# A small weight matrix at the head of a fused scan and mixture-of-adapters kernel: loaded in 64-byte pieces, or in 8 rows and transposed on TensorE

## The chip, the cores and the metric

One core of one Trainium2 chip. The metric is the device time of one execution in microseconds (us); lower is better. The profiled execution is one more run of the same program.

## What is computed

The reference, cut to what matters. `a` and `b` are 8 x 6400 x 128; the result of the scan is 51200 rows of 128, and each row goes through the two best of eight low-rank adapters.

```python
def _attn_ref(a, b):                      # a, b: (8, 6400, 128)
    for t in range(S):
        h = a[:, t] * h + b[:, t]
        out[:, t] = h

def _moe_ref(x, w_gate, A, B):            # x: (51200, 128), w_gate: (128, 8)
    logits = x @ w_gate                   # A: (8, 128, 16), B: (8, 16, 128)
    topk = np.argpartition(-logits, K, axis=1)[:, :K]      # K = 2
    ...                                   # w: softmax over the two
    for e in range(E):
        for k in range(K):
            mask = topk[:, k] == e
            z = x[mask] @ A[e]
            delta[mask] += w[mask, k, None] * (z @ B[e])
    return x + delta
```

## The kernel before

The 51200 rows are cut into 100 units of 512. One unit v goes through these steps; the names are those of the kernel's plan:

- `AB{v}` (line 86, TensorE): `a` and `b` of the unit are transposed in fp32 against `ident_f` into PSUM (`pA`, `pB`), so that time runs along the free axis. Units 0 and 1 and the last are special: where a tile is loaded alone, four 128x128 transposes do what eight 64-row transposes do elsewhere, and the `a` part is then a step of its own, `A{v}`, in front of the `b` part.
- `aev{v}` (line 491, ScalarE): `pA` is copied to SBUF.
- `scan{v}` (line 510, VectorE): the recurrence, 512 steps for 128 channels at once, out in fp16 into the ring `xT`.
- `L{v}` (line 82, into `pTL`): logits, four matmuls against the fp16 gate weights. `lev`, `mx` (MAX8, line 589), `p1` to `p7`, `sig`: the gate of a group of one to four units, on ScalarE, VectorE and GpSimd.
- `Z{v}` (line 82, into `pZ`): four matmuls against `Acat_h`, moe_A as one 128x128 fp16 matrix (row d, column e*16+r).
- `mul{v}` (line 729), `T{v}` (line 86), `tev{v}` (line 786): z times its gate, transposed, copied back.
- `R{v}` and `D{v}` (line 82, into `pO`): x itself through `ident_h`, and the adapters' second matrix `Bcat_h`, summed in PSUM. `oev{v}` (line 821): copied to SBUF, then stored.

SyncE (SP) issues all loads of `a` and `b` and all stores; ScalarE's queue issues the three small loads of the weights (`ld_g`, `ld_A`, `ld_B`, by `cst_load`). The casts of the weights to fp16 (`cstg`, `cstA`, `cstB`) run on GpSimd. At the start TensorE has nothing to do until the first tile lands; `heat` gives it seven 512-column matmuls on zeros, and `fill0` three more behind unit 0's transposes.

The order on each engine is fixed when the program is built. `_Plan.schedule` keeps for every step a cost (time on the engine, time to its end) and what it depends on, and goes through the engines in planned time: at each turn the engine that can start soonest takes, among its steps that can start within a small slack (20 ns on TensorE and VectorE, 0 on ScalarE), the one with the smallest key. The key is the unit's number plus an offset for the kind of step: -228.9 for `AB`, -12.2 for `L`, 27.8 for `Z`, 83.5 for the gate, 140.1 for `scan`; steps of the kind `fix` have their number alone (-109 to -105 for the set-up, 1000 for the filler). A change of the tile mode on TensorE ("half", "full") is planned at 94 ns. So a cost or a dependency changed in one place can change the order on all engines behind it. Waits on semaphores follow from the dependencies, also for one step of an engine on an earlier one of the same engine.

TensorE's program is cut into parts by `_Parts`: the first holds 172 entries, each later one 243; a matmul or transpose counts as two. At a cut the engine's sequencer branches to the next part.

Of the kernel before, what the change touches and what calls it, by code (L numbers as in the profile page):

```python
# [91 lines left out]
class _Plan:  # L92
# [9 lines left out]
    def add(self, name, eng, kind, unit, cost, emit, deps=(), dma=None, bank=None, mode=None):  # L102

        engs = (eng,) if isinstance(eng, str) else eng
        cost = cost if isinstance(cost, dict) else {e: cost for e in engs}
        self.ops[name] = _Op(name, engs, kind, unit, cost, emit, list(deps), dma, bank, mode)
# [98 lines left out]
def bass_associative_scan_2x2__then__mixture_of_adapters_kernel(  # L205
# [9 lines left out]
    E = moe_w_gate.shape[1]  # L215
    R = moe_A.shape[2]
# [33 lines left out]
    with ExitStack() as stack:  # L250
        sb = stack.enter_context

        ident_f = sb(nc.sbuf_tensor("ident_f", [128, 128], F32))
        ident_h = sb(nc.sbuf_tensor("ident_h", [128, 128], F16))
        cst_f = sb(nc.sbuf_tensor("cst_f", [128, E + 256], F32))
# [4 lines left out]
        Acat_h = cst_h[:, E : E + 128]  # L260
# [5 lines left out]
        A_e = sb(nc.sbuf_tensor("A_e", [E, D * R], F32))  # L266
# [25 lines left out]
        pZ = [sb(nc.psum_tensor(f"pZ{i}", [128, UT], F32)) for i in range(NZ)]  # L292
# [7 lines left out]
        add = plan.add  # L300

        def add_dma(name, eng, unit, starts, slot, time, deps=()):
# [6 lines left out]
            def emit(h):  # L309
# [18 lines left out]
                fill=1.0,  # L328
# [7 lines left out]
        def cst_load(name, dst, src, after):  # L336

            sem = sb(nc.semaphore(f"s_{name}"))
            add(
                name,  # L340
                "act",
                "fix",
                -109,
                (450.0, 0.0),
                lambda h: h.dma_start(dst, src).then_inc(sem, 16),
                after,
                (sem, 16, 100.0),
            )

        cst_load("ld_g", cst_f[:, 0:E], moe_w_gate[:, :], [])  # L350
        cst_load(
            "ld_A",
            cst_f[:, E : E + 128].rearrange("d (e r) -> d e r", e=E),
            moe_A.rearrange("e d r -> d e r"),
            [],
        )
        cst_load("ld_B", cst_f[:, E + 128 : E + 256], moe_B.rearrange("e r d -> (e r) d"), [])
        add("w0", "dve", "fix", -109, (60.0, 200.0), lambda h: h.memset(warm[:, :], 0.0))
        add("table", "act", "fix", -108, (1500.0, 1600.0), lambda h: h.activation(warm[:, :], warm[:, :], ACTF.Sigmoid), ["w0"])
# [9 lines left out]
        def fill(w):  # L369


            def emit(h):
                for _ in range(3):
                    last = h.matmul(pO[1][:, :], warm_t[:, 0:128], warm_t[:, :])
                return last

            add(f"fill{w}", "pe", "fix", 1000.0, (600.0, 800.0), emit, [f"AB{w}"])

        for w in range(FILLS):
            fill(w)  # L380
        add("idh", "dve", "fix", -108, (150.0, 330.0), lambda h: h.tensor_copy(ident_h[:, :], ident_f[:, :]), ["id"])
        add("cstg", "pool", "fix", -108, (190.0, 290.0), lambda h: h.tensor_copy(wg_h, cst_f[:, 0:E]), ["ld_g"])
        add(
            "cstA",
            "pool",
            "fix",
            -107,
            (290.0, 390.0),
            lambda h: h.tensor_copy(Acat_h, cst_f[:, E : E + 128]),
            ["ld_A"],  # L390
        )
        add(
            "cstB",
            "pool",
# [532 lines left out]
```

## Time and profile before

| | |
|---|---|
| median of 3 runs | 204.48 us (204.47 to 204.71) |
| profiled execution | 204.28 us |
| its span in the profile | 202.5 us |
| TensorE, VectorE, ScalarE, GpSimd busy | 191.0, 184.7, 174.0, 115.7 us |
| granted TensorE clock | 1.00 |
| HBM traffic | 78.8 MB, 389 GB/s over the span |

The profiled execution's own time is 1.8 us longer than its span, since what lies ahead of the first and behind the last instruction is not in the span. In the rows of the profile, PE is TensorE's matmul, PEld its weight load, DVE is VectorE, ACT ScalarE, POOL GpSimd, SP SyncE; a q behind the name is the engine's queue. A timeline row gives start, duration, engine, line, operation, out<-in, shapes, count, and in brackets the idle time in front and what ended it.

### The profile page before, as it was taken

What the parts mean: (1) busy time and instruction counts of PE and PEld (TensorE: products, weight loads), DVE (VectorE), ACT (ScalarE), POOL (GpSimd) and SP (SyncE); (2) the same over time, 40 slices, a digit from 0 to 9 for tenths busy, and PEclk for the clock granted to TensorE, in tenths of its full rate; (3) what the DMA queues carried; (4) which work ended last, traced back from release to release, by engine and by line L of the source; (5) the groups of instructions that cost most, each with busy time, mean ns of one, the idle gap of its engine ahead of it and who ended that gap; (6) DMA issues with size and microseconds to landing.
All of it is one profiled execution on the core that took longest, in us unless ns stands there. A gap on an engine that the chain in (4) does not pass through costs nothing.

```text
span 202.5 us, 8763 instructions
## 1 busy us (share of the span) xinstructions
PE 191.0 (94%) x3594; PEld 171.4 (85%) x3594; DVE 184.7 (91%) x268; ACT 174.0 (86%) x383; POOL 115.7 (57%) x244
## 2 busy tenths in 40 slices
PE   7888988899999999999999999999999999999982
PEld 3666777789899999999999999999999999998981
DVE  1699989999999999999999999999999999988970
ACT  2366775969999999999999999999999999999882
POOL 1325337668467565656746656565674687865620
PEclk9999999999999999999999999999999999999999
DMA  7999999999999999999999999999999999988866
GB/s 185 401 408 409 406 408 406 403 406 411 403 413 414 410 419 409 409 411 414 412 416 409 414 413 411 411 415 415 409 412 414 413 414 410 385 350 350 324 271 263
DMA packets 23687, 79.35 MB, mean 392 GB/s; under 512 B 3680, under 2 KB 3808, under 8 KB 23648
## 3 DMA queue, kind: packets, MB, share of 16 engines
q1 hardware_dynamic: 22320, 78.65, 97.3%
q8 instruction: 29, 0.48, 1.0%
q10 hardware_dynamic: 1328, 0.14, 0.5%
q14 instruction: 10, 0.08, 0.1%
HBM read 52.56 MB, written 26.21 MB: 389 GB/s over the span
## 4 chain that ended last, share of the span: by engine, by line
PE 84%; ACT 6%; DVE 5%; issue 2%; POOL 1%; DVEq 0%
PE pA L86 27%; PE pO L82 23%; PE pTL L86 14%; PE pZ L82 10%; PE pTL L82 5%; DVE xT L510 4%; PE pB L86 4%; ACT a_st L491 2%; ACT outt L821 2%; PE pB L82 2%; ACT zwT L786 1%; DVE mx L589 1%; ACT Lg L583 0%; ACT z_sb L715 0%; POOL pn L632 0%
## 5 line engine op out<-in xcount | busy, mean ns | idle before, releaser
L510 DVE TENSOR_TENSOR_SCAN xT<-a_st,xT,pB 128x512 f16<-128x512 f32 x96 | 120.1, 1251 | 3.2 <-ACT zwT L786 0.5
L491 ACT COPY a_st<-pA 128x512 f32<-128x512 f32 x100 | 60.6, 606 | 19.2 <-PE pB L86 14.6
L86 PE MATMUL pA<-ident_f,a_in 64*128 64x64 f32 (+1 forms) x792 | 71.8, 230 | 2.5 <-ACT a_st L491 0.7
L86 PE MATMUL pB<-ident_f,b_in 64*128 64x64 f32 (+1 forms) x792 | 71.9, 230 | 0.3 <-issue 0.2
L86 PEld LDWEIGHTS pA<-ident_f,a_in 64*128 64x128 f32 (+1 forms) x792 | 57.9, 139 | 10.9 <-ACT a_st L491 1.9
L821 ACT COPY outt<-pO 128x512 f32<-128x512 f32 x96 | 59.5, 626 | 1.9 <-PE pO L82 1.7
L786 ACT COPY zwT<-pTL 128x512 f16<-128x512 f16 x95 | 58.4, 615 | 1.0 <-PE pTL L86 1.0
L86 PEld LDWEIGHTS pB<-ident_f,b_in 64*128 64x128 f32 (+1 forms) x792 | 57.5, 138 | 1.0 <-issue 0.7
L729 DVE TENSOR_TENSOR zw<-pZ,g 128x512 f16<-128x512 f32 x79 | 53.2, 679 | 2.4 <-PE pTL L86 1.4
L82 PE MATMUL pO<-ident_h,xT 128*128 128x128 f16 x400 | 40.8, 227 | 0.9 <-ACT outt L821 0.9
L86 PE MATMUL pTL<-ident_h,zw 128*128 128x128 f16 x380 | 37.8, 221 | 0.5 <-ACT zwT L786 0.4
L82 PE MATMUL pZ<-cst_h,xT 128*128 128x128 f16 x400 | 38.1, 219 | 0.0
L82 PE MATMUL pO<-cst_h,zwT 128*128 128x128 f16 x400 | 36.8, 218 | 0.5 <-ACT zwT L786 0.4
L82 PEld LDWEIGHTS pO<-ident_h,xT 128*128 128x128 f16 x400 | 32.5, 147 | 1.5 <-ACT outt L821 1.2
L729 POOL TENSOR_TENSOR zw<-z_sb,g 128x512 f16<-128x512 f32 x21 | 22.3, 1060 | 17.8 <-PE pTL L82 17.3
L82 PE MATMUL pTL<-cst_h,xT 128*128 128x8 f16 x400 | 27.5, 174 | 1.4 <-DVE xT L510 1.3
L82 PEld LDWEIGHTS pZ<-cst_h,xT 128*128 128x128 f16 x400 | 27.8, 114 | 0.1
L86 PEld LDWEIGHTS pTL<-ident_h,zw 128*128 128x128 f16 x380 | 21.8, 98 | 6.7 <-ACT zwT L786 0.5
L625 POOL TENSOR_TENSOR d<-Lg,m 128x128 f32<-128x128 f32 (+3 forms) x29 | 10.7, 369 | 26.6 <-DVE m L618 26.5
L82 PEld LDWEIGHTS pTL<-cst_h,xT 128*128 128x128 f16 x400 | 23.5, 117 | 2.6 <-DVE xT L510 2.0
L82 PEld LDWEIGHTS pO<-cst_h,zwT 128*128 128x128 f16 x400 | 23.8, 98 | 1.0 <-PE pO L82 0.9
L660 POOL TENSOR_SCALAR pn<-d 128x128 f32<-128x128 f32 (+3 forms) x31 | 17.3, 557 | 2.7
(38 smaller groups left out, 138.3 us busy)
## 6 DMA issues: line engine op xcount, KB each, us to landing
a_in<-in_a_dram SPq DMA_DIRECT2D x49, 512.0 KB, 14.4
b_in<-in_b_dram SPq DMA_DIRECT2D x49, 512.0 KB, 14.2
out_dram<-outt SPq DMA_DIRECT2D x47, 512.0 KB, 13.9
out_dram<-outt SPq DMA_DIRECT2D x6, 256.0 KB, 3.0
a_in<-in_a_dram SPq DMA_DIRECT2D x2, 256.0 KB, 9.1
b_in<-in_b_dram SPq DMA_DIRECT2D x2, 256.0 KB, 4.1
cst_f<-in_moe_A_dram ACTq DMA_DIRECT2D x1, 64.0 KB, 4.2
cst_f<-in_moe_B_dram ACTq DMA_DIRECT2D x1, 64.0 KB, 4.9
```

Of the source, the lines that this page charges most:

```text
L82: return self.h.matmul(*args, **kw)
L86: return self.h.transpose(*args)
L491: lambda h: h.copy(a_st[w % 2][:, :], pA[0][:, :]),
L510: last = h.tensor_tensor_scan(out=x_at(lo, hi), data0=a_st[w % 2][:, lo:hi], data1=pB[w % 2][:, lo:hi], initial=init, op0=ALU.mult, op1=AL ...
L589: last = h.max(mx[s][:, j, :], Lg[s][:, j, :])
L625: lambda h: h.tensor_tensor(out=v(d1[s]), in0=v(Lg[s]), in1=bc(m1[s]), op=ALU.subtract),
L660: lambda h: h.tensor_scalar(v(pn[s]), v(d2[s]), 0.0, -1.0e30, ALU.is_lt, ALU.mult),
L729: lambda h: h.tensor_tensor(out=oview, in0=zview, in1=gview, op=ALU.mult),
L786: lambda h: h.copy(*evacuated(v)),
L821: return copy(outt[:, v % NOUT, :], pO[v % NO][:, :])
```

## The change

moe_A is (8, 128, 16). Before, one DMA puts it straight into place as 128 rows by (e, r), in pieces of 16 floats (64 bytes), and GpSimd casts it. Now the DMA brings it as it lies, 8 rows of 2048 floats, into `A_e` (which both kernels declare), and TensorE transposes, for each r, the 8 x 128 slice with stride 16 into a 128 x 8 slice of `pZ[1]`, again with stride 16 (`arrange`, step `cstT`). The step waits for `ld_A`, the identity and unit 0's last transpose (`AB0`), and has the tile mode "few". VectorE casts the result from PSUM into `Acat_h`. The filler `fill0` has one matmul instead of three, and its planned cost goes from 600 to 200 ns.

```diff
         cst_load("ld_g", cst_f[:, 0:E], moe_w_gate[:, :], [])
-        cst_load(
-            "ld_A",
-            cst_f[:, E : E + 128].rearrange("d (e r) -> d e r", e=E),
-            moe_A.rearrange("e d r -> d e r"),
-            [],
-        )
+        cst_load("ld_A", A_e[:, :], moe_A.rearrange("e d r -> e (d r)"), [])
...
             def emit(h):
-                for _ in range(3):
+                for _ in range(1):
                     last = h.matmul(pO[1][:, :], warm_t[:, 0:128], warm_t[:, :])
                 return last
 
-            add(f"fill{w}", "pe", "fix", 1000.0, (600.0, 800.0), emit, [f"AB{w}"])
+            add(f"fill{w}", "pe", "fix", 1000.0, (200.0, 300.0), emit, [f"AB{w}"])
...
-        add(
-            "cstA",
-            "pool",
-            "fix",
-            -107,
-            (290.0, 390.0),
-            lambda h: h.tensor_copy(Acat_h, cst_f[:, E : E + 128]),
-            ["ld_A"],
-        )
+        def arrange(h):
+            dst = pZ[1][:, 0:128].rearrange("d (e r) -> d r e", e=E)
+            src = A_e[:, :].rearrange("e (d r) -> e r d", r=R)
+            for r in range(R):
+                last = h.transpose(dst[:, r, :], src[:, r, :], ident_f[0:E, 0:E])
+            return last
+
+        add("cstT", "pe", "fix", -105, (600.0, 700.0), arrange, ["ld_A", "id", "AB0"], mode="few")
+        add("cstA", "dve", "fix", -107, (150.0, 330.0), lambda h: h.tensor_copy(Acat_h, pZ[1][:, 0:128]), ["cstT"])
```

## The prediction

> **What bounds the kernel now.** I read the page first (busy shares, the chain that ended last), then the busy time by stretch, then who waited for whom, then the timeline of the first 12 us, where the whole change lies.
>
> ```profile
> span 202.5 us, 8763 instructions
> PE 191.0 (94%) x3594; PEld 171.4 (85%) x3594; DVE 184.7 (91%) x268; ACT 174.0 (86%) x383; POOL 115.7 (57%) x244
> PE 84%; ACT 6%; DVE 5%; issue 2%; POOL 1%; DVEq 0%
> ...
> 10.00:57.00 47.00, 42.34 (x810) 36.72 (x808) 45.40 (x74) 35.86 (x81) 25.34 (x58) 1.00 1.03 407
> 57.00:180.00 123.00, 122.91 (x2444) 113.56 (x2444) 120.12 (x162) 117.86 (x261) 79.87 (x155) 1.00 1.02 410
> ```
>
> In a stretch row the columns after its length are busy PE, PEld, DVE, ACT and POOL, then clock, DMA share and GB/s. From 57 to 180 us PE has no hole (122.91 of 123.00). From 10 to 57 it has 4.7 us of holes, and there VectorE (DVE) is the fullest engine, 45.40 of 47.00. So two engines take turns as the bound, both close to full: whatever makes DVE start its unbroken run later makes PE start its own later too, and nothing behind has room to make it up except the few stops that DVE still has:
>
> ```profile
> DVE mx L589 <- ACT Lg L583: 1.0, 1, 1.0
> DVE xT L510 <- ACT zwT L786: 0.5, 1, 0.5
> DVE zw L729 <- PE pTL L86: 0.2, 1, 0.2
> DVE xT L510 <- PE pO L82: 0.2, 1, 0.2
> ```
>
> These are all of DVE's waits from 8 to 57 us: 1.0 at the very start (it is in front of the first MAX8) and 0.9 in three stops later. DMA is full too (share 1.03), but no row of the waits from 8 us on has a PE that waits for a DMA.
>
> The head, PE first, then DVE:
>
> ```profile
> 4.18 0.94 PE L86 MATMUL pA<-ident_f,a_in 128*128 128x128 f32 x4
> 5.27 0.63 PE L86 MATMUL pB<-ident_f,b_in 128*128 128x128 f32 x4
> 5.96 0.82 PE L82 MATMUL pO<-warm_t 128*128 128x512 f16 x3
> 6.19 0.59 PE L82 MATMUL pO<-warm_t 128*128 128x512 f16 x2
> 6.40 0.38 PE L82 MATMUL pO<-warm_t 128*128 128x512 f16 x1
> 6.71 0.57 PEld L86 LDWEIGHTS pA<-ident_f,a_in 64*128 64x128 f32 x8 [0.42 <-issue]
> 6.71 0.71 PE L86 MATMUL pA<-ident_f,a_in 64*128 64x64 f32 x8
> 7.35 0.29 PE L82 MATMUL pTL<-cst_h,xT 128*128 128x8 f16 x4
> 7.57 0.63 PE L86 MATMUL pB<-ident_f,b_in 128*128 128x128 f32 x4
> 8.03 0.39 PE L82 MATMUL pZ<-cst_h,xT 128*128 128x128 f16 x4
> 8.26 0.39 PE L82 MATMUL pO<-ident_h,xT 128*128 128x128 f16 x4
> ...
> 5.94 1.22 DVE L510 TENSOR_TENSOR_SCAN xT<-a_st,pB 128x512 f16<-128x512 f32 x1 [4.21 <-PE pB L86]
> 8.16 0.37 DVE L589 MAX8 mx<-Lg 128x8 f32<-128x8 f32 x4 [1.00 <-ACT Lg L583]
> 8.45 1.26 DVE L510 TENSOR_TENSOR_SCAN xT<-a_st,xT,pB 128x512 f16<-128x512 f32 x1
> ```
>
> The chain reads: unit 0's b transposes (5.27 to 5.90), three fillers, unit 1's a transposes (6.71, in the text A1), unit 0's logits, unit 1's b transposes (B1, to 8.20), then scan 1. The three fillers start 0.21 apart (5.96 in the longer rows, 6.19, 6.40), and A1 starts 0.31 behind the third: 0.21 of matmul and about 0.1 that I put down to the change of tile size. A1 is held by PE alone: its data had landed.
>
> ```profile
> 1.65 0.42 SPq L311 DMA_DIRECT2D a_in<-in_a_dram  x1
> ...
> a_in<-in_a_dram SPq DMA_DIRECT2D x1, 512.0 KB, 4.7
> cst_f<-in_moe_A_dram ACTq DMA_DIRECT2D x1, 64.0 KB, 4.2
> ...
> DMA packets 1109, 0.26 MB, mean 262 GB/s; under 512 B 1048, under 2 KB 1048, under 8 KB 1109
> q10 hardware_dynamic: 1032, 0.07, 70.7%
> ...
> 5.45 0.29 POOL L389 CAST cst_h<-cst_f 128x128 f16<-128x128 f32 x1 [1.47 <-DMA cst_f<-in_moe_A_dram]
> ```
>
> Issued at 1.65, landed 4.7 later: 6.35, against A1 at 6.71.
>
> **The change part by part.**
>
> *The load of moe_A.* The packet rows are for 3.5 to 4.5 us: queue 10 moves 1032 packets, nearly all moe_A's 64-byte pieces, and they take 70.7% of 16 engines for 1.0 us, 0.71 us. Eight rows of 8 KB are the same 64 KB; at the 407 GB/s of the stretch row that is 0.16 us, or 0.32 if only half of the engines work on it. So the loads behind it land 0.4 to 0.55 us sooner. I value that at nothing: A1's data was there at 6.35 and is now there sooner, and later PE does not wait for loads. moe_A itself landed by 5.45; the transposes can start only behind unit 0's, at 5.96, so even the old landing would do. One issue on ACT's queue stays one issue.
>
> *Fillers, three to one.* Takes 2 x 0.21 = 0.42 us off PE between unit 0 and A1.
>
> *Sixteen transposes.* They wait for unit 0's last transpose, as the first filler does now, so they start at 5.96; by the planner's costs the remaining filler follows them and A1 follows that. Queued behind them on PE: A1, the logits of unit 0, B1, and so everything. The price of one is not in the trace (8 rows, 8 columns moving, fp32, weights read 64 bytes apart). From below: the paired 64-row transposes of unit 2 start 16 within half a microsecond (first and last below), 33 ns apart, but they alternate between two halves of the array, which these cannot. From above: the weights of the group that reads xT 16 bytes apart take 147 ns against 98 for those that read a tile straight; 1.5 times.
>
> ```profile
> 8.59 0.26 PE L86 MATMUL pA<-ident_f,a_in 64*128 64x64 f32 x1
> 9.08 0.22 PE L86 MATMUL pB<-ident_f,b_in 64*128 64x64 f32 x1
> ...
> L82 PEld LDWEIGHTS pO<-ident_h,xT 128*128 128x128 f16 x400 | 32.5, 147 | 1.5 <-ACT outt L821 1.2
> L82 PEld LDWEIGHTS pO<-cst_h,zwT 128*128 128x128 f16 x400 | 23.8, 98 | 1.0 <-PE pO L82 0.9
> ```
>
> The nearest row is A1 itself: eight fp32 transposes in one part of the array, their weight loads 0.57 us, 71 ns each. The ends are 33 and 1.5 x 71 = 107 ns; I take 71, because the number of weight columns (128) is the same and the 16-byte stride, dear for one load, does not slow the group: four of them take 0.39 at 8.26, like the four at 8.03. [...]
>
> So 5.96 + 16 x 0.071 = 7.10, tile change 0.1, filler 0.21, tile change 0.1: A1 at about 7.5 instead of 6.71, 0.8 later (0.2 later at 33 ns, 1.4 at 107).
>
> *The cast.* It moves from POOL to DVE, reading PSUM. DVE's cast of a 128x128 tile takes 0.23 (row below). It lies in the idle time between scan 0, which ends at 7.16, and scan 1, and the matmuls that need it (Z0) come behind B1: nothing. If that idle time were gone it would cost 0.23.
>
> ```profile
> 1.50 0.23 DVE L381 CAST ident_h<-ident_f 128x128 f16<-128x128 f32 x1 [0.34 <-POOL ident_f L324]
> ```
>
> *The order.* The kernel sorts its instructions by a plan, and unit 1 is now later in it. Worked by hand with the plan's own costs, the a transposes of unit 1 slip by 186 ns and its b transposes by 126; unit 0's first gate step, in front of scan 1 by 19 ns until now, comes 41 ns behind it. So I expect scan 1 ahead of the four MAX8, and with unit 0's gate later, its zw product behind scan 3 rather than scan 2. That moves work about on DVE and adds none worth counting. Also the PE program is cut into parts; 14 more instructions (16 transposes less two fillers) move every cut. A cut inside a burst shows at 18.95 to 19.18: 0.23 between pairs that otherwise start 0.06 apart.
>
> ```profile
> 18.95 0.22 PE L86 MATMUL pA<-ident_f,a_in 64*128 64x64 f32 x1
> 19.18 0.27 PE L86 MATMUL pA<-ident_f,a_in 64*128 64x64 f32 x1
> ```
>
> The first cut falls behind the first transpose of unit 3: 0.17 at most, into the range.
>
> *The sum.* B1 ends at 8.20 + 0.8 = 9.0, scan 1 starts 0.04 later, as scan 0 did after its own. DVE's idle time behind scan 0 grows from 1.00 to 1.9: 0.9 us late at the head of the stage in which it is the bound, and PE, full from 57 on, starts that run 0.9 late. The profiled execution took 204.28 us, 1.78 more than its span; the median of the three runs is 204.48. 204.28 + 0.9 = 205.2 for a profiled run like this one, 204.48 + 0.9 = **205.4 us** for the median. At 33 ns scan 1 starts at 8.4, idle 1.25, so 204.7; at 107 ns 9.6, idle 2.4, so 205.9.
>
> **The rivals.**
>
> *The stops close (faster).* DVE has 0.9 us of stops behind 8.16, which come from the order of gate, copies and transposes. If the new order closes them, and the transposes run at 33 ns, the end is 204.48 + 0.25 - 0.9 = 203.8. For: the stops are single events. Against: all three end with ACT or PE steps, which shift along. It decides from a shift of under 0.5 us.
>
> *The stops swallow it (no change).* The same at 71 ns: 204.48 + 0.9 - 0.9 = 204.5.
>
> *Strided weights are dear (slower).* 107 ns: 205.9.
>
> *The clock falls back.* The seven matmuls before 4.39 took 3.17 us, the three fillers 0.82: 0.45 against 0.27 each, and unit 0's first four transposes 0.94 against 0.63 for the next. PE speeds up at about 5 us, although the granted clock column says 1.00. If 16 tiny transposes in place of two fillers let it fall back, some 3.5 us of PE work up to 10 us takes 1.65 times as long: 2.3 more, 207.7. Against: PE still has work in every slice.
>
> ```profile
> 1.22 3.17 PE L82 MATMUL pB<-warm_t 128*128 128x512 f16 x7 [1.22 <-DVE warm_t L360]
> 6.00:8.00 2.00, 2.00 (x19) 1.39 (x20) 1.16 (x1) 0.54 (x2) 0.29 (x1) 1.00 1.05 406
> 8.00:10.00 2.00, 1.53 (x32) 1.30 (x31) 1.71 (x6) 0.72 (x3) 1.02 (x4) 1.00 1.03 414
> ```
>
> [...]
>
> **How the numbers follow.** The forecast 0.54, the stops close 0.20, the stops swallow it 0.10, strided weights 0.10, the clock 0.06. A measurement of this kernel can tell about 0.2%, 0.41 us, from no change, so the band is 204.07 to 204.89. The forecast's low end (transposes near 33 ns) lies in it: 0.04 of its 0.54. Faster 0.20, same 0.14, slower 0.66. Range: from 203.8, below which half of the fast case lies, to 206.1, the dear transposes and a cut; above it is the clock case: about 0.16 left out.
>
> **What would show it.** The 16 transposes between unit 0 and one filler, 1.1 us together; A1 at 7.5; the cast on DVE before 8; scan 1 at 9.0 and ahead of MAX8; landings of the first loads 0.4 us sooner with no effect; PE full from about 58 on. Wrong: A1 at 7.0 or before; scan 1 as early as 8.5; DVE's 10-to-57 share above 46 of 47; matmuls 0.4 apart again after 6 us.

## The result, and the profile after

The kernel after takes **210.68 us** (median of four runs, 209.63 to 211.53); the kernel before, run beside it, 204.47 (204.45 to 204.71). The ratio is 1.030, with a 95% interval from 1.025 to 1.035. The prediction said 205.4 us and at most 206.1: the sign is right, the size is not. Of 6.2 us lost it foresaw 0.9. (The ratios and intervals in this document leave out single runs that took over 1.5% more than the fastest run of the same kernel.)

The profiled execution took 210.45 us. From its page, and then its busy time by stretch (columns as before):

```profile
span 208.7 us, 8790 instructions
PE 195.4 (94%) x3608; PEld 175.2 (84%) x3608; DVE 185.1 (89%) x271; ACT 173.9 (83%) x383; POOL 115.0 (55%) x241
q8 instruction: 30, 0.49, 0.9%
```

```profile
10.00:57.00 47.00, 42.11 (x769) 36.35 (x769) 43.54 (x76) 33.12 (x76) 23.17 (x55) 1.00 1.03 406
57.00:180.00 123.00, 122.86 (x2444) 113.48 (x2442) 120.39 (x162) 117.83 (x259) 79.03 (x150) 1.00 1.02 408
```

From 57 us on nothing has changed; PE is full as before (122.86 of 123.00). The loss is ahead of that and behind it. The table sets the start times of the same steps side by side (from the timelines, us):

| | scan 0 | scan 1 | scan 2 | scan 3 | scan 8 | scan 30 | scan 60 | last scan | last `outt` copy | last store landed |
|---|---|---|---|---|---|---|---|---|---|---|
| before | 5.94 | 8.45 | 10.01 | 12.07 | 21.21 | 57.54 | 110.12 | 187.22 | 198.57 | 201.6 |
| after | 6.62 | 11.49 | 14.08 | 16.62 | 25.37 | 61.45 | 114.14 | 191.48 | 203.19 | 207.8 |
| later by | 0.68 | 3.03 | 4.07 | 4.55 | 4.16 | 3.92 | 4.02 | 4.26 | 4.62 | 6.2 |

(The first scan is scan 0.) So 4.07 us are lost before scan 2 and carried to the end with little change (3.9 to 4.6), and 1.6 us more are lost behind the last copy. First the head, PE's timeline:

```profile
5.47 1.11 PE L86 MATMUL pB<-ident_f,b_in 128*128 128x128 f32 x4 [0.23 <-DMA b_in<-in_b_dram]
6.73 1.90 PE L86 MATMUL pZ<-ident_f,A_e 8*128 8x8 f32 x16
8.56 0.61 PE L82 MATMUL pO<-warm_t 128*128 128x512 f16 x1
9.10 1.11 PE L86 MATMUL pA<-ident_f,a_in 64*128 64x64 f32 x8
10.36 1.09 PE L86 MATMUL pB<-ident_f,b_in 128*128 128x128 f32 x4
11.24 0.63 PE L82 MATMUL pZ<-cst_h,xT 128*128 128x128 f16 x4
...
13.76 0.39 PE L82 MATMUL pO<-ident_h,xT 128*128 128x128 f16 x4
```

Unit 0's four b transposes take 1.11 us where they took 0.63, A1 1.11 for 0.71, B1 1.09 for 0.63, Z0 0.63 for 0.39. At 13.76 four matmuls take 0.39 again. PE ran at half speed until some 13.4 us (experiment 4, at a recorded clock of 0.50, has the same 1.11, 1.09 and 0.63); before, it sped up at about 5. Unit 0's b transposes stand ahead of the sixteen small ones, so in this run the clock did not fall because of these: it had not risen yet, and it stayed low. The clock column of the page reads full speed here all the same: the trace's record of the granted clock begins with the first full stretch, at 13.67 us (before: at 4.86), and what has no record is printed as full. In this head the clock has to be read from the time that a known instruction takes.

DVE behind it:

```profile
6.62 1.22 DVE L505 TENSOR_TENSOR_SCAN xT<-a_st,pB 128x512 f16<-128x512 f32 x1 [4.89 <-PE pB L86]
8.67 0.29 DVE L386 CAST cst_h<-pZ 128x128 f16<-128x128 f32 x1 [0.83 <-PE pZ L86]
11.49 1.28 DVE L505 TENSOR_TENSOR_SCAN xT<-a_st,xT,pB 128x512 f16<-128x512 f32 x1 [2.53 <-PE pB L86]
12.69 0.35 DVE L584 MAX8 mx<-Lg 128x8 f32<-128x8 f32 x4
14.08 1.28 DVE L505 TENSOR_TENSOR_SCAN xT<-a_st,xT,pB 128x512 f16<-128x512 f32 x1 [0.72 <-ACT Lg L578]
16.01 0.69 DVE L724 TENSOR_TENSOR zw<-pZ,g 128x512 f16<-128x512 f32 x1
16.62 1.27 DVE L505 TENSOR_TENSOR_SCAN xT<-a_st,xT,pB 128x512 f16<-128x512 f32 x1
```

DVE has nothing to do from 8.96 to 11.49: it waits 2.53 us for B1. It is the same path as before, longer by the sixteen transposes (6.73 to 8.56) and slower.

The loads, in the lists of DMA issues up to 6 us (KB each, us from issue to landing), before and then after:

```profile
b_in<-in_b_dram SPq DMA_DIRECT2D x2, 256.0 KB, 4.1
a_in<-in_a_dram SPq DMA_DIRECT2D x1, 256.0 KB, 2.8
cst_f<-in_moe_B_dram ACTq DMA_DIRECT2D x1, 64.0 KB, 4.9
```

```profile
b_in<-in_b_dram SPq DMA_DIRECT2D x2, 256.0 KB, 5.1
a_in<-in_a_dram SPq DMA_DIRECT2D x1, 256.0 KB, 3.0
cst_f<-in_moe_B_dram ACTq DMA_DIRECT2D x1, 64.0 KB, 5.8
```

The first loads land 0.2 to 1.0 us later, not 0.4 sooner.

### The profile page after: what moved, and what is told of

It is laid out like the page before. It is cut to its first block, busy times and chain, and to the rows that moved or that the text cites. A ratio compares the mean times of both kernels' runs of the same rounds, so it can differ in the third digit from the quotient of the medians.

```text
span 208.7 us, 8790 instructions
## 1 busy us (share of the span) xinstructions
PE 195.4 (94%) x3608; PEld 175.2 (84%) x3608; DVE 185.1 (89%) x271; ACT 173.9 (83%) x383; POOL 115.0 (55%) x241
## 4 chain that ended last, share of the span: by engine, by line
PE 85%; ACT 6%; DMA 2%; issue 2%; DVE 2%; SPq 0%; DVEq 0%
PE pA L86 28%; PE pO L82 24%; PE pTL L86 14%; PE pZ L82 10%; PE pTL L82 5%; PE pB L86 4%; ACT a_st L486 2%; DMA b_in<-in_b_dram 2%; DVE xT L505 2%; ACT outt L816 2%; ACT zwT L781 1%; PE pZ L86 1%; ACT Lg L578 0%; ACT z_sb L710 0%; ACT g L679 0%
## 5 line engine op out<-in xcount | busy, mean ns | idle before, releaser
L86 PE MATMUL pA<-ident_f,a_in 64*128 64x64 f32 (+1 forms) x792 | 72.7, 232 | 2.0 <-ACT zwT L781 0.7
L86 PE MATMUL pB<-ident_f,b_in 64*128 64x64 f32 (+1 forms) x792 | 73.0, 232 | 0.4 <-DMA b_in<-in_b_dram 0.2
L86 PEld LDWEIGHTS pA<-ident_f,a_in 64*128 64x128 f32 (+1 forms) x792 | 58.6, 140 | 10.4 <-issue 2.0
L86 PEld LDWEIGHTS pB<-ident_f,b_in 64*128 64x128 f32 (+1 forms) x792 | 58.4, 140 | 1.1 <-DMA b_in<-in_b_dram 0.6
L82 PE MATMUL pO<-ident_h,xT 128*128 128x128 f16 x400 | 41.5, 229 | 1.2 <-ACT outt L816 0.9
```

The costliest lines, as they stand in the source:

```text
L82: return self.h.matmul(*args, **kw)
L86: return self.h.transpose(*args)
```

## The experiments

Every kernel but the first and the eleventh is the kernel before with one edit. `PART0` goes up or down in them by two for each matmul or transpose that the edit adds to PE's program or takes from it, so that the program is cut behind the same instruction as before, and the order of the rest is the same. Where work is added to PE (experiments 4 to 10 and 12), GpSimd also sets `A_e` to zeros at the head, and the filler step waits for it, or in experiment 6 for `ident_h`. The cuts from the code are shown in part: against experiment 4 in experiments 5, 8, 9 and 12, against 7 in 10, and against the kernel after in 1 and 11. Each experiment is set against runs of the kernel before that were made beside it: 204.31 us in the median for experiments 1 to 4, 204.68 for 5 to 7 and 13, 204.36 for 8 to 11, 204.55 for 12 and 14.

**1. The cuts put back** (the kernel after)

```diff
-PART0 = 172
+PART0 = 200
```

> The changed kernel with the first part of TensorE's program 200 entries long instead of 172, so that every later cut stands where it stood before the change. Cuts theory: the 30th program fetch of 16 KB, which came at 203.9 us beside the last stores, is gone, the last store lands about 1.5 us sooner: 209.2 us. Clock, loads and transposes theories: they lie in the head and are untouched, 210.7 us.

Measured: 209.4 us (207.49 to 209.77, four runs), ratio to before 1.023 (1.017 to 1.029): 1.3 less than the kernel after. The two intervals overlap (that of the kernel after is 1.025 to 1.035), so the times alone don't settle it; the traces do better. Its page has 29 program fetches, like the page before, for 30 in the kernel after. The end of both in the lists of DMA issues from 200 us on, the kernel after first:

```profile
q8 instruction: 1, 0.02, 0.6%
...
out_dram<-outt SPq DMA_DIRECT2D x4, 256.0 KB, 4.2
```

```profile
out_dram<-outt SPq DMA_DIRECT2D x4, 256.0 KB, 2.4
```

The thirtieth fetch (16 KB, 0.95 us of one DMA engine) comes at 203.9 us, when the last stores are on their way. One engine's packets trail until 207.4 while the others are done at 205.7. Without it the four stores land in 2.4 instead of 4.2 us, and from the last copy to the last landing there are 2.8 us instead of 4.6 (before: 3.0). The last 1.6 us of the table are this, by one trace of each kernel.

The same run shows the clock as it goes, in its busy time by stretch (the clock is the third column from the end):

```profile
4.20:7.40 3.20, 2.61 (x22) 2.16 (x21) 1.22 (x1) 0.59 (x1) 0.19 (x1) 1.00 1.02 374
7.60:14.20 6.60, 6.60 (x65) 5.45 (x66) 2.92 (x9) 1.35 (x4) 1.12 (x4) 0.50 1.03 412
14.50:17.60 3.10, 1.96 (x38) 1.48 (x34) 2.88 (x10) 1.91 (x5) 0.83 (x3) 1.00 1.03 411
17.90:21.10 3.20, 3.20 (x44) 2.90 (x44) 3.12 (x12) 1.85 (x4) 0.90 (x3) 0.50 1.03 405
21.30:57.00 35.70, 31.66 (x607) 27.48 (x604) 33.16 (x46) 26.87 (x60) 20.27 (x45) 1.00 1.02 405
```

Full, half, full, half, full. In this trace's own record of the granted clock the first four stretches last 3.41, 6.83, 3.41 and 3.41 us: one, two, one and one times 3.41. Here, unlike in the profile of the kernel after, the clock rose early (at 4.1) and then fell (at 7.5), while the sixteen transposes ran (6.06 to 7.89). The moment of its first rise differs between profiles with the same warming matmuls (4.02 to 5.55 us in experiments 1 to 7).

**2. One filler instead of three, nothing else**

```diff
-                for _ in range(3):
+                for _ in range(1):
```

> The kernel before with one filler matmul instead of three, same plan and same cuts. Fillers theory (the two fillers taken away are what lets TensorE's clock stay low): matmuls behind 6 us stay 0.2 apart, 206 to 208 us. Rival (the clock rises by what ran before 4.9 us, fillers do not matter): two fillers less on the path, 204.1 to 204.5 us.

Measured: 204.38 us (204.21 to 204.87, ten runs), ratio 0.9999 (0.9987 to 1.0012). Two fillers less cost nothing and bring nothing; in its trace the clock stays at full from 5.5 us on.

**3. The load by rows, without the transposes**

```diff
+        cst_load("ld_A", A_e[:, :], moe_A.rearrange("e d r -> e (d r)"), [])
+        add("zA", "dve", "fix", -100, (150.0, 330.0), lambda h: h.memset(cst_f[:, E : E + 128], 0.0))
```

The old load is gone; moe_A is loaded by rows but not used, and the adapters get zeros in its place, so their part of the output is left out.

> The kernel before with moe_A loaded as 8 rows of 8 KB into A_e and not used (the fp16 weights come from zeros, so the adapters are left out), no transposes, three fillers, order as before. Loads theory (eight engines are held 0.65 us each, the first tiles land 1 us late): unit 0's b at 5.4, unit 1's a at 7.35 instead of 6.35, A1 0.65 late, 205.1 to 205.6 us. Clock theory alone (transposes or fillers): 204.5 us. If the late tiles are also what leaves the clock low: 207 or more.

Measured: 204.7 us (204.41 to 205.37 in ten runs), ratio 1.0018 (1.0007 to 1.0029): 0.4 us. The loads that come later are worth 0.1 to 0.6 us in these ten runs. The eleventh, the profiled one, took 207.52 us and is not in them. Its trace shows more than its time. Unit 1's `a` landed late, PE stood idle for it, and the clock was at half for 6.83 us, with no small transposes at all:

```profile
8.76 1.09 PE L86 MATMUL pA<-ident_f,a_in 64*128 64x64 f32 x8 [1.85 <-DMA a_in<-in_a_dram]
```

```profile
5.30:8.60 3.30, 1.45 (x7) 0.63 (x7) 1.22 (x1) 0.57 (x1) 0.00 (x0) 1.00 0.95 346
8.70:15.40 6.70, 6.61 (x72) 5.74 (x72) 3.44 (x8) 1.69 (x6) 1.32 (x5) 0.50 1.03 417
```

This is one run in eleven, and it shows no cause; it says that the clock can be lost here without the small transposes.

**4. The sixteen transposes alone**, on a tile of zeros, ahead of the three fillers

```diff
+                dst = pZ[1][:, 0:128].rearrange("d (e r) -> d r e", e=E)
+                src = A_e[:, :].rearrange("e (d r) -> e r d", r=R)
+                for r in range(R):
+                    h.transpose(dst[:, r, :], src[:, r, :], ident_f[0:E, 0:E])
                 for _ in range(3):
```

> The kernel before with 16 transposes of 8 x 128 added in front of the three fillers, of zeros that are in place early, result not used; load, casts and order as before, first part 204 entries so that cuts stand. Transposes theory with the clock up: 16 at about 65 ns, A1 1.1 late, 205.4 us. If the transposes themselves keep or take the clock down: over 207 us, with matmuls 0.2 apart behind them.

Measured: 208.74 us (208.21 to 209.12, four runs), ratio 1.022 (1.020 to 1.025): 4.4 us, with the old load, the old order and the old cuts. Timeline of PE, and busy time by stretch:

```profile
5.53 1.92 PE L86 MATMUL pZ<-ident_f,A_e 8*128 8x8 f32 x16
7.39 1.46 PE L82 MATMUL pO<-warm_t 128*128 128x512 f16 x3
8.77 1.11 PE L86 MATMUL pA<-ident_f,a_in 64*128 64x64 f32 x8
```

```profile
4.10:7.40 3.30, 3.09 (x26) 2.62 (x25) 1.22 (x1) 0.59 (x1) 0.58 (x2) 1.00 1.07 376
7.50:14.20 6.70, 6.70 (x57) 4.90 (x58) 2.20 (x7) 1.46 (x5) 1.03 (x4) 0.50 1.03 409
14.30:57.00 42.70, 37.56 (x721) 32.38 (x720) 40.69 (x68) 31.65 (x71) 22.40 (x53) 1.00 1.03 406
```

Two things stand here: from 5.53 to the filler at 7.39 the sixteen take 1.85 us, 116 ns each; and behind them the clock is at half for 6.83 us, the fillers take 1.46 us for 0.82. Note that PE is busy in 3.09 of 3.30 us ahead of the fall. Being busy did not hold the clock.

**5. Sixteen transposes of full size** in their place, 128x128

```diff
-                    h.transpose(dst[:, r, :], src[:, r, :], ident_f[0:E, 0:E])
+                    h.transpose(pZ[1][:, r % 4 * 128 : r % 4 * 128 + 128], ident_f[:, :], ident_f[:, :])
```

> The kernel before with sixteen full transposes (128x128, fp32, the identity by itself) ahead of the three fillers, where the run with sixteen 8-row ones took 208.74 us. Leaves out nothing. Theory 1, transposes of any size do not hold the clock: matmuls behind unit 0 start 0.4 us apart for some 7 us, and the time is 208 us or more (the full transposes themselves take up to 16 x 0.157 = 2.5 us at the full clock, by the 0.63 us of four at 5.27). Theory 2, only the small ones, which use 8 rows of the array, let it fall: the clock stays, A1 starts 16 x 0.11 to 0.157 = 1.8 to 2.5 us later than before, and the time is 206.2 to 207.0.

PE's timeline:

```profile
6.09 1.97 PE L86 MATMUL pZ<-ident_f 128*128 128x128 f32 x16
7.89 0.81 PE L82 MATMUL pO<-warm_t 128*128 128x512 f16 x3
```

Measured: 206.56 us (206.39 to 207.10, four runs), ratio 1.010 (1.008 to 1.013). They take as long as the small ones (6.09 to 7.89), the clock stays at full (0.995 to 0.999 on the mean in all four runs, 0.974 to 0.992 in experiment 4), and the time is 2.2 us less than with the small ones, or 2.5 less when each is set against its own runs of the kernel before. With sixteen big transposes in the place of sixteen small ones the clock held.

**6. Twenty plain matmuls of the small size**, fp16, no transposes

```diff
+                for r in range(20):
+                    h.matmul(pZ[1][:, r * 8 : r * 8 + 8], ident_h[0:E, :], ident_h[0:E, 0:E])
```

> The kernel before with twenty plain matmuls of the same small size (8 rows, 128 columns of weights, 8 columns moving, fp16) ahead of the three fillers, no transposes; their output is used by nothing. Theory 1, only transposes let the clock fall: it stays at full, A1 starts about 20 x 0.05 = 1.0 us later, 205.3 us. Theory 2, any work on so small a part of the array lets it fall: 208 us or more, with matmuls 0.4 us apart behind it.

Measured: 206.19 us (205.78 to 206.31, four runs), ratio 1.008 (1.005 to 1.010), between the two expectations. The trace says why, in the timeline and in PE's waits from 25 to 60 us:

```profile
6.01 0.65 PE L82 MATMUL pZ<-ident_h 8*128 8x8 f16 x20
6.60 0.82 PE L82 MATMUL pO<-warm_t 128*128 128x512 f16 x3
```

```profile
PE pO L82 <- issue: 1.0, 1, 1.0
```

The clock stays; scan 1 is 0.64 us late, as the twenty matmuls are long. Near 50 us PE then stands still for 1.0 us and waits for nothing that is shown; scan 30 is 2.06 late. What that stop is was not tried. As to the question whether small matmuls, too, let the clock fall, twenty of these were too short (0.6 us) to tell the theories apart; experiment 8 is the longer one.

**7. The fillers spread among the transposes**, ahead of the 1st, 6th and 12th

```diff
+                for r in range(R):
+                    if r in (0, 5, 11):
+                        h.matmul(pO[1][:, :], warm_t[:, 0:128], warm_t[:, :])
+                    last = h.transpose(dst[:, r, :], src[:, r, :], ident_f[0:E, 0:E])
```

> The same work as the run that took 208.74 us (sixteen 8-row transposes and three fillers), but the fillers stand ahead of the first, the sixth and the twelfth transpose. Theory 1, the clock falls when a stretch of a few us holds transposes and too few matmuls: the fillers keep it, so about 16 x 0.07 = 1.1 us of added work and 205.4 us. Rival, the added instructions cost by their own length and the order of DVE behind them: 208.7 us again.

Measured: 206.33, 208.52, 208.62 and 210.46 us, with a mean granted clock of 1.000, 0.983, 0.982 and 0.970. No answer in the median, but a clear one run by run: with the clock at full all along, the sixteen transposes cost 1.65 us (206.33 against 204.68); the two runs at 0.982 and 0.983 take 2.2 to 2.3 more, and the trace of one of them (208.62) has a single fall of 6.83 us, from 8.2 to 15.0. The fourth run has no trace. Why the clock falls in one run of this kernel and holds in another is not shown.

**8. The same operands, plain fp32 matmuls instead of transposes**

```diff
-                    h.transpose(dst[:, r, :], src[:, r, :], ident_f[0:E, 0:E])
+                    h.matmul(dst[:, r, :], src[:, r, :], ident_f[0:E, 0:E])
```

> As the run of before with sixteen 8-row transposes (208.74 us), but the same operands are multiplied by plain fp32 matmuls instead of being transposed. Theory 1, it is the transpose as a kind of work that does not hold the clock: it stays at full, A1 starts 16 x 0.116 = 1.85 us later than before, 206.4 us. Theory 2, what counts is how many columns are moved through how many rows in a window of 3.41 us, and these move as few: the clock falls in most runs, 208.5 us, matmuls 0.4 apart behind them.

PE's timeline, and the busy time of the stretch behind the fall:

```profile
5.60 7.10 PE L82 MATMUL pZ<-ident_f,A_e 8*128 8x8 f32 x32
12.63 1.46 PE L82 MATMUL pO<-warm_t 128*128 128x512 f16 x3
```

```profile
7.60:24.50 16.90, 16.45 (x146) 13.99 (x147) 6.92 (x16) 3.53 (x10) 2.34 (x9) 0.50 1.02 408
```

Measured: 216.18 us (215.03 to 217.05, four runs). Each fp32 matmul is two instructions of 0.22 us, so they take 7.0 us, much more than expected. But the clock falls at 7.56, as it did with the transposes, after 1.96 us of them, and stays at half until 24.6. So it is not the transpose as a kind of work. What experiments 4 and 8 share is work that moves 8 columns through 8 rows at a time; whether the few columns or the few rows matter was not tried apart.

**9. The same transposes without the step of 64 bytes**

```diff
-                    h.transpose(dst[:, r, :], src[:, r, :], ident_f[0:E, 0:E])
+                    h.transpose(pZ[1][:, r * E : r * E + E], A_e[:, r * 128 : r * 128 + 128], ident_f[0:E, 0:E])
```

> The same sixteen 8-row transposes, but each reads a contiguous 128 columns and writes a contiguous 8, instead of stepping 64 bytes on both sides; their output is used by nothing. If the step is what makes one cost 116 ns: 50 to 71 ns each, 0.8 to 1.1 us together, and as the three fillers then come sooner in the same window the clock is held more often: 205.5 us where it is held, 208 where not. If the step costs nothing: 116 ns again and 208.7 us.

PE's timeline:

```profile
5.93 1.15 PE L86 MATMUL pZ<-ident_f,A_e 8*128 8x8 f32 x16
7.01 0.82 PE L82 MATMUL pO<-warm_t 128*128 128x512 f16 x3
```

Measured: 205.70, 205.77, 206.05 and once 209.18 us, ratio 1.007 (1.004 to 1.010). The sixteen now take 1.08 us, 67 ns each. So the step costs 49 ns on each, which of the two sides (SBUF read or PSUM write) was not tried apart. In three runs the clock is at 0.997 to 0.999 and the time short; in the trace of one the three fillers behind the sixteen take 0.82 us, as at full clock. The fourth (209.18) also reads 1.000, but that mean says nothing of a late first rise, and the run has no trace: what made it long is open.

**10. Five fillers spread among the sixteen**

```diff
-                    if r in (0, 5, 11):
+                    if r in (0, 3, 6, 9, 12):
```

> As the run with three fillers among the sixteen transposes (206.33 to 210.46 us), but with five, ahead of the 1st, 4th, 7th, 10th and 13th. [...] Theory 1 (the transposes themselves, whatever stands between them): falls again, 208.6 to 210.9.

Measured: 207.68 us with the clock at 1.000, and 209.77 to 209.85 in four other runs, with 0.980 to 0.982. By theory 2 of experiment 8 the author's estimate was a clock held in every run, at 206.3 + 2 x 0.21 = 206.8 us; it was held in one of five. The 207.68 is 0.9 over that sum, too: three transposes and a filler repeat every 0.74 us, 0.56 by their own times. (Experiment 7's timeline has 1.07 us from the filler at 6.88 to the one at 7.95, with 0.21 + 6 x 0.116 = 0.91 by their own times.) The difference is put down, as an estimate, to the two changes of the tile around each filler. (Only the 207.68 has a trace; that the clock fell in the other four is read from the mean.)

**11. The kernel after, mended**: the cuts put back, and a filler ahead of every fourth transpose

```diff
-PART0 = 172
+PART0 = 208
...
             for r in range(R):
+                if r % 4 == 0:
+                    h.matmul(pO[1][:, :], warm_t[:, 0:128], warm_t[:, :])
                 last = h.transpose(dst[:, r, :], src[:, r, :], ident_f[0:E, 0:E])
```

> The kernel after with two things mended: the cuts of the PE program back behind the same instructions as before (29 program fetches), and four more fillers, one ahead of every fourth transpose. If the clock, the fetch and the transposes' own time are all there is: 204.5 + 1.85 (sixteen transposes at 116 ns) + 0.4 (the load by rows) + 0.43 (five fillers for three) = 207.2 us. If something else of the change costs: 208.5 or more with the clock at full.

Measured: 207.67 us in the one run with the clock at 1.000; 210.17, 211.30 and 211.81 with 0.970 to 0.972. Where the clock holds, the time is 0.5 over the sum, which the changes of the tile can account for as in experiment 10 (an estimate: four more fillers among the transposes, at 0.18 each, are 0.7); that is one run. As a mending it fails.

**12. Eight transposes instead of sixteen**

```diff
-                for r in range(R):
+                for r in range(8):
```

> The run of before with added 8-row transposes, but eight of them instead of sixteen (208.74 us) ahead of the three fillers. [...] Rival, each transpose costs its share of the 4.4 us wherever it stands: 8 x 0.27 = 2.2 us more, 206.5 us.

PE's timeline:

```profile
5.96 1.04 PE L86 MATMUL pZ<-ident_f,A_e 8*128 8x8 f32 x8
6.94 0.82 PE L82 MATMUL pO<-warm_t 128*128 128x512 f16 x3
```

Measured: 205.47 us (204.82 to 205.62 in nine runs, one of 208.20), ratio 1.003 (1.002 to 1.005). With the clock held, the author's estimate was 8 x 0.116 + 0.1 = 1.0 us more, 205.4 us. Half the transposes cost 0.9 us, a fifth of what sixteen cost (4.4). The cost is not in proportion: there is a step between eight and sixteen, and by the two traces it is the clock, which holds with eight (mean 0.999, the fillers in 0.82 us) and falls with sixteen (0.981, in 1.46).

**13 and 14. Six warming matmuls instead of seven**

```diff
-HEATS = 7
+HEATS = 6
```

> The kernel before with six instead of seven matmuls ahead of unit 0's first transpose; nothing else. If the clock still rises at about 5 us: unit 0's transposes start up to 0.43 us earlier, 204.1 us. If the seventh is needed for the rise: the clock rises a window later or falls back, 207 us or more. If unit 0's data, which land at about 4.5 us, hold the transposes: no change.

> The kernel before with six warming matmuls again, with more rounds, as the only version so far that may beat both: 204.34 us, ratio 0.9988 (0.9976 to 1.0001) in three rounds. If the 0.43 us that unit 0 starts sooner reach the end: ratio 0.998 or less with its interval below 1. If unit 1's loads hold them back: 1.000.

Measured: ratio 0.9988 (0.9976 to 1.0001), then 0.9996 (0.9982 to 1.0011) with more rounds: no difference. In the profile of the first, A1 waits for its load, which is the old one (PE idle 1.38 us, until 7.54); in that of the second the clock rises only at 6.50, unit 0's b transposes take 1.09 us, and the time is still 204.59:

```profile
5.05 1.09 PE L86 MATMUL pB<-ident_f,b_in 128*128 128x128 f32 x4
6.20 0.95 PE L82 MATMUL pO<-warm_t 128*128 128x512 f16 x3
7.08 0.71 PE L86 MATMUL pA<-ident_f,a_in 64*128 64x64 f32 x8
```

So no version here beats the kernel before.

**What the 6.2 us are.** By the medians: sixteen transposes by their own length, 16 x 0.116 = 1.85; the clock behind them, 4.4 - 1.85 = 2.55 (experiment 4); the load by rows, 0.4 (3); the thirtieth fetch, 1.3 (1); two fillers less, 0 (2). Together 6.1, of 6.2. That it closes so well is partly luck. The 1.3 is the difference of two medians whose intervals overlap. And the 2.55 holds something else: in the trace of experiment 4 scan 2 is 3.73 us late, in that of experiment 5, where the sixteen take as long and the clock stays at full, 1.91, so that the fall is worth 1.8 there. In both a further 0.6 us comes up between scans 16 and 22 (3.75 to 4.37, and 1.91 to 2.54); it is neither the clock nor the transposes, its cause was not tried, and the kernel after doesn't have it (3.93 to 4.01). So the clock is worth 1.8 to 2.6 us. The changed order was not tried by itself. The nearest to it is experiment 11, with the clock at full and the thirtieth fetch gone: 0.5 us over the sum, in one run. In the trace of the kernel after, the 0.4 us between the last scan and the last copy are not explained either.

**What decides the clock** is not shown; the runs narrow it down. Being busy is not enough: in experiment 4 PE is busy in 3.09 of 3.30 us ahead of the fall. It is not the transpose as a kind of work: sixteen of 128 rows held the clock (experiment 5, fillers in 0.81 us), and plain matmuls on the operands of the small ones let it fall (experiment 8). Between experiments 4 and 5 the time spent is the same (1.85 and 1.80 us) and the work moved is not: by the shapes in their rows sixteen times 8 columns through 8 rows, against sixteen times 128 through 128. The profiled run of experiment 3 lost the clock with PE busy in only 1.45 of 3.30 us ahead of the fall, with little moved, too. Theory 2 of experiment 8, that the work moved is what counts, agrees with these runs and with experiment 12; how much work would be enough is not shown. Two things it leaves open. In experiment 10 the clock fell in four of five runs although more was moved than in experiment 7. And the first rise came at 4.86 us in the kernel before and at 13.67 in the kernel after, behind the same seven warming matmuls (1.22 to 4.39 in both) and the same eight transposes of unit 0, and at 6.50 with six of them in experiment 14.

## Why the prediction was wrong, and where it was right

- **What bounds the kernel**: right. DVE and PE take turns close to full, and a late start goes to the end: 4.07 us late at scan 2, 4.26 at the last scan. The stops did not close.
- **The clock**: this is the step that failed. It stood as a rival with a chance of 0.06 and a price of 2.3 us. What it describes happened, at about that price (1.8 to 2.6): experiment 4 shows that the sixteen are enough to let the clock fall, and experiment 1, the same kernel with its cuts put back, shows the fall at 7.5 us. In the profiled run of the kernel after, the clock had not risen yet and stayed low until 13.4, to the same effect; why its first rise did not come, before the sixteen began, is open. The argument against it, "PE still has work in every slice", was no argument: in experiment 4 PE is busy in 3.09 of 3.30 us ahead of the fall, and in 6.70 of 6.70 behind it while the clock stays at half. The runs speak for how much the work moves as what counts: sixteen transposes of 8 columns through 8 rows let the clock fall (experiment 4), sixteen of 128 through 128, as long, did not (5). The test that the prediction set, "matmuls 0.4 apart again after 6 us", is met in experiment 4 (fillers at 7.39 in 1.46 us). The fillers, of which it thought two lost, were not the cause: without them alone nothing changed (experiment 2), with them the clock fell all the same (4).
- **Sixteen transposes**: 116 ns each, not 71, above even the upper end of 107. The step that failed is the sentence that a stride does not slow a group; without the stride they take 67 (experiment 9, which takes the step off both sides at once). They take as long at both clocks: 1.85 us for the sixteen at full (experiment 4), 1.83 at half in the kernel after (6.73 to 8.56). The row that the prediction weighed and set aside, a weight load of 147 ns at a 16-byte step against 98 for a straight one, pointed the right way. With 116 ns the prediction's own sum would have been about 206.0 (205.9 at 107 ns, and 16 x 0.009 more).
- **The load of moe_A**: the sign was wrong. 64 KB in eight rows should have freed 0.4 us of the DMA engines; each of the eight packets of 8 KB took 0.58 to 0.80 us of one engine in the kernel after (0.31 to 0.59 in the three other traces with this load), and loads behind them landed 0.2 to 1.0 us later. In all that is 5.2 us of one engine, where the 1024 pieces took 11.3, and still the loads came later; why was not tried. What was right is that it matters little: 0.4 us (experiment 3).
- **The cut**: "0.17 at most" looked at the stall at one place. The fourteen instructions more also make a thirtieth fetch, at the very end, where the stores run: 1.3 us by the medians, 1.6 by the traces.
- **The order**: scan 1 went ahead of MAX8 as worked by hand. Unit 0's zw product is at 16.01, ahead of scan 3 and not behind it. What the order cost was not measured by itself.
- **The cast**: right in that it costs nothing; 0.29 us on DVE at 8.67, later than "before 8" but in idle time.
- **The range**: it took the cases one at a time. What happened is the clock's case together with three terms that were sized too small (the transposes, the load, the cut).

## What to carry to other kernels

In these runs being busy did not hold TensorE's clock: behind sixteen 8-row transposes, with PE busy in 3.09 of 3.30 us, it was at half for 6.83 us (experiment 4), and with plain matmuls of the same operands for 17.07 us (experiment 8), while sixteen 128-row transposes in their place held it (experiment 5); and with a path that nothing behind makes up, such a loss goes to the end (4.07 us late at scan 2, 4.26 at the last scan). Read the clock at the head from how long a known instruction takes (1.11 us for 0.63 in the kernel after), not from the clock column (1.00 there). When a change adds instructions, count the program fetches (30 for 29 here) and look where the last one falls (203.9 us, beside the last stores); and a load in few long rows wasn't faster here for having fewer packets (8 for 1024, and the loads behind them landed 0.2 to 1.0 us later).

## What was not expected of the hardware

- In the clock records of these traces the granted clock changed only at multiples of 3.41 us from its first rise: stretches of 3.41 and 6.83 us in experiment 1, 6.83 in 3, 4 and 7, 17.07 and 27.3 in 8; the full stretches of the kernel before and the kernel after, 197.97 and 191.15 us, differ by 6.83. And the same kernel took 206.33 us with the clock at 1.000 and 208.5 to 208.6 with it at 0.982 to 0.983 (experiment 7).
- An 8-row fp32 transpose that steps 64 bytes took 116 ns at the full clock (experiment 4) and 114 at the half (kernel after, 1.83 us for sixteen), a 128-row one that reads straight 112 (experiment 5, 6.09 to 7.89 for sixteen), an 8-row one that reads straight 67 (experiment 9).
- With a 16 KB program fetch beside them (203.9 us, kernel after) the last four stores landed in 4.2 us in the median, without it (experiment 1) in 2.4.
- Eight 8 KB packets took 0.58 to 0.80 us each on their engines in the kernel after, 0.31 to 0.59 in other traces; 1024 pieces of 64 bytes had taken about 11 ns each.
